# A scheduled attention and feed-forward kernel: a written order in place of a list scheduler, other places for the filler matmuls, and a last tile cut 384 and 128

## The chip, the core and the metric

The kernel runs on one core of a Trainium2 chip. The metric is the device time of one execution in microseconds (us); lower is better. Engines are named as the profile names them: PE is TensorE, PEld its weight loads, DVE is VectorE, ACT is ScalarE, POOL is GpSimd, SP is SyncE, which here only issues transfers.

## What is computed

Eight batches of eight heads, 576 tokens of 64 numbers each, go through two attentions and a feed-forward layer. First the 32 learned queries `p` attend to `k` and `v`; then `q` attends to the 32 results. The heads are laid side by side to a matrix of 4608 tokens by 512, which goes through `w_in` (512 by 2048), an activation and `w_out` (2048 by 512).

```python
def sm_attn(qq, kk, vv):
    s = scale * np.matmul(qq, kk.transpose(0, 1, 3, 2))
    a = np.exp(s - np.max(s, axis=-1, keepdims=True))
    a = a / (np.sum(a, axis=-1, keepdims=True) + 1e-09)
    return np.matmul(a, vv)
p_packed = sm_attn(p, k, v)
x = heads_side_by_side(sm_attn(q, p_packed, p_packed))
h = x @ w_in
g = np.where(h >= 1, h, np.where(h <= -1, 0.0, (h + 1) ** 2 / 4))
out = g @ w_out
```
(`heads_side_by_side` stands for a transpose and a reshape.)

## The kernel before

**The stages.** Each batch goes through the same steps, in tiles whose names are those of the profile. `tp` transposes `k` and `q` on PE for batches 0 and 1; later batches use DMA transposes that SP issues (`kT`, `qT`, L626). `sp` are the scores of `p`, `ex` their exponentials (ACT), `pk` the packed values and their sums, `rs` a reciprocal (DVE), `ppT` the packed values as bf16. `s` are the scores of `q`, `eT` their exponentials (ACT), `sm` their sums, `ln` and `rc` the reciprocal by logarithm and exponential (ACT), `A` the normalized weights (DVE). `mp` is the packed values times `w_in`, and `M` its bf16 copy (ACT or DVE, L333), so that the feed-forward layer's first product is `h = A·M` (L939). Each batch has 16 blocks of 128 columns of `d_ff`, numbered `fi`, and each block makes `h`, then `x` (ACT, L945), `t` (DVE L953 or ACT L955) and `hT` (DVE, L960). The output `o` (L1030) adds up 16 matmuls, one for each `fi`, into a tile of 128 tokens by 512; `ob` is its copy (L333, ACT or DVE) and L1058 stores it, in two pieces, since a tile's tokens lie in two places of the output. Two batches share nine output tiles, so tile `o1.3` is tile 3 of the second pair. The very last tile, `o3.8`, is computed and stored as two halves of 256 columns.

**What sets the order.** Every step is a task of class `Plan` with the engines that could run it, a duration on each, the tasks that it depends on and the buffers that it takes. `run` is a list scheduler: at each turn it takes, over all engines, a ready task that can start first, among those within 0.05 us by the lowest rank, and a free choice of engine falls to whichever is free. Ranks are due times in table `RANKS`. The result is sorted by planned start, and the code of all tasks is issued in that order; each engine then runs its own instructions in that order, and waits where data or a buffer is not there yet. PSUM slots for `h`, `mp`, `s`, `sm`, `tp` and `sp` come from a pool of three (`w`), those of `o` from a pool of two, and `ob` has four buffers.

**The filler matmuls.** Before the first `o`, PE is given matmuls on a tile of zeros (`o<-zeros`, L1108, 512 or 256 columns) in the planned gaps between its tasks. A list `fill` holds for each planned gap the planned time at which it begins and the number of matmuls, and the loop that issues the code puts them ahead of the first task, of any engine, that is planned to start later than that:

```python
    for t in order:
        while fill and t.start > fill[0][0] and t is not consts:
            warm(fill.pop(0)[1])
        t.ways[t.engine][2](t.engine)
```

Of the kernel before, what the change touches and what calls it, by code (L numbers as in the profile page):

```python
# [24 lines left out]
class Plan:  # L25
# [5 lines left out]
    CLAIM = 0.3  # L31
# [8 lines left out]
    def add(self, rank, ways, deps=(), takes=(), mode=None, behind=(), name=None, late=0.0):  # L40
        n = self.count[name]
        self.count[name] += 1
        if name in self.ranks:
            rank = float(self.ranks[name][min(n, len(self.ranks[name]) - 1)])
        t = Task(rank, ways, deps, takes, mode, behind, name, late)
        self.tasks.append(t)
        return t
# [7 lines left out]
    def run(self, slack):  # L55
        waiting = {id(t): len(t.deps) + len(t.behind) for t in self.tasks}
        for t in self.tasks:
            for d in t.deps + t.behind:
                d.users.append(t)
        ready = [t for t in self.tasks if not waiting[id(t)]]  # L60
        done = []
        while ready:
            best = None
            for claims in (True, False):
                found = defaultdict(list)
                left = {b: sorted(v) for b, v in self.slots.items()}
                for t in sorted(ready, key=lambda t: t.rank):
                    at = max((d.end + self.LATENCY for d in t.deps), default=0.0) + t.late
                    at = max([at] + [d.start + 0.001 for d in t.behind])
                    need = defaultdict(int)  # L70
                    for b in t.takes:
                        need[b] += 1
                    short = any(len(left[b]) < n for b, n in need.items())
                    wants = claims and at < self.free["PE"] + self.CLAIM
                    for b, n in need.items():
                        if not short:
                            at = max(at, left[b][n - 1] + self.LATENCY)
                        if wants:
                            del left[b][:n]
                    if short:  # L80
                        continue
                    for e in t.ways:
                        found[e].append((max(self.free[e], at), t))
                for e, some in found.items():
                    first = min(x[0] for x in some)
                    at, t = min((x for x in some if x[0] <= first + slack.get(e, 0.0)), key=lambda x: (x[1].rank, x[0]))
                    if best is None or at < best[0]:
                        best = at, t, e
                if best is not None:
                    break  # L90
            assert best is not None, "no step can take its buffers"
            at, t, e = best
            if e == "PE" and t.mode != self.mode:
                at = max(at, self.free[e] + self.SWITCH)
            ready.remove(t)
            keep, lasts = t.ways[e][:2]
            t.start, t.engine = at, e
            if e == "DMA":
                begin = max(self.pipe, at + lasts)
                self.pipe = begin + t.ways[e][3]  # L100
# [11 lines left out]
            if e == "PE":  # L112
                self.mode = t.mode
            for b in t.takes:
                self.slots[b].remove(min(self.slots[b]))
# [15 lines left out]
def kernel(  # L131
# [10 lines left out]
    nc = tc.nc  # L142
# [1001 lines left out]
```

## Time and profile before

| what | value |
|---|---|
| median of 3 runs | 241.63 us (241.58 to 241.64) |
| profiled execution, first to last instruction (span) | 240.4 us |
| median less span | 1.2 us |
| mean granted TensorE clock | 0.998 |
| PE busy | 233.2 us (97%) |
| ACT busy | 190.0 us (79%) |
| DVE busy | 179.4 us (75%) |
| POOL busy | 37.7 us (16%) |
| zero matmuls | 42, of them 36 of 512 columns and 6 of 256 |

The profiled execution shows its span alone; the time of a run holds 1.2 us more than that span, before the first instruction and behind the last. A share of busy time is an average over the whole span. The first 22 us are a start-up, in which loads land and the first batch goes through a chain of short steps; the rest is a steady stage in which PE alternates between `h` and `o`; the last microseconds are a copy and a store.

### The profile page before, as it was taken

The numbers are of one execution on the slowest core, as the hardware profiler recorded it, in microseconds if no ns is written. First come the engines' busy times: TensorE is split into PE (matmuls) and PEld (weight loads), VectorE is DVE, ScalarE is ACT, GpSimd is POOL, SyncE is SP. The second block draws the span as 40 slices with busy tenths as digits, with TensorE's granted clock in tenths as the row PEclk, the third lists the DMA queues.
The fourth block names the chain that finished last, engine by engine and source line by source line (L and its number), as shares of the span: only waits on it lengthen the run. The fifth ranks groups of instructions, "written<-read, shape, count | busy, mean of one in ns | idle before, by whom it ended". The sixth has DMA issues, their size and how long they took to land.

```text
span 240.4 us, 5315 instructions
## 1 busy us (share of the span) xinstructions
PE 233.2 (97%) x2096; PEld 133.9 (56%) x2096; DVE 179.4 (75%) x320; ACT 190.0 (79%) x324; POOL 37.7 (16%) x57
## 2 busy tenths in 40 slices
PE   7799999999999999999999999999999999999993
PEld 3555565565555655466546655656456554654452
DVE  4549997499977996699868989999469967995000
ACT  3578898799989986899889898998789886984211
POOL 8552306000510040070005000300000000000000
PEclk9999999999999999999999999999999999999999
DMA  7999999999999999999999997989301210111315
GB/s 155 201 206 207 203 202 206 199 257 171 148 188 248 186 171 204 187 174 213 204 183 197 218 213 117 138 189 203 97 2 48 74 33 27 44 40 52 98 45 119
DMA packets 65353, 36.42 MB, mean 152 GB/s; under 512 B 34480, under 2 KB 60848, under 8 KB 65328
## 3 DMA queue, kind: packets, MB, share of 16 engines
q0 software_dynamic: 28080, 18.26, 53.5%
q1 hardware_dynamic: 36544, 17.28, 33.4%
q10 hardware_dynamic: 704, 0.56, 0.8%
q8 instruction: 16, 0.26, 0.4%
q14 instruction: 9, 0.07, 0.1%
HBM read 37.22 MB, written 9.44 MB: 194 GB/s over the span
## 4 chain that ended last, share of the span: by engine, by line
PE 92%; ACT 3%; DMA 2%; DVE 1%; issue 0%
PE o L1030 51%; PE h L939 26%; PE mp L792 3%; DMA k_raw<-in_k_dram 2%; PE o L1108 2%; PE pk L730 2%; PE sm L835 2%; PE sp L652 2%; PE s L770 1%; PE tp L564 1%; ACT M L333 1%; PE pk L740 1%; DVE M L333 0%; ACT rc L846 0%; PE tp L601 0%; PE sp L667 0%
## 5 line engine op out<-in xcount | busy, mean ns | idle before, releaser
L1030 PE MATMUL o<-w_out_sb,hT 128*128 128x512 bf16 (+1 forms) x592 | 146.3, 374 | 0.0
L960 DVE SCALAR_TENSOR_TENSOR hT<-t 128x576 bf16<-128x576 f32 (+1 forms) x130 | 91.9, 742 | 3.7 <-ACT t L955 2.1
L945 ACT ACTIVATE x<-h 128x576 f32<-128x576 f32 (+1 forms) x130 | 79.2, 646 | 11.6 <-PE h L939 10.7
L1030 PEld LDWEIGHTS <-hT 128*128 128x128 bf16 x592 | 55.3, 98 | 49.3 <-issue 5.6
L939 PE MATMUL h<-A,M 128*128 128x288 bf16 x512 | 78.1, 286 | 0.6 <-ACT M L333 0.4
L939 PEld LDWEIGHTS <-M 128*128 128x128 bf16 x512 | 49.6, 98 | 27.7 <-issue 1.5
L953 DVE TENSOR_SCALAR t<-x 128x576 f32<-128x576 f32 (+1 forms) x75 | 33.6, 463 | 10.6 <-ACT x L945 10.2
L955 ACT ACTIVATE t<-x 128x576 f32<-128x576 f32 (+1 forms) x55 | 37.0, 684 | 0.9
L333 ACT COPY ob<-o 128x512 f32<-128x512 f32 (+1 forms) x21 | 11.9, 567 | 16.5 <-PE o L1030 16.3
L851 DVE SCALAR_TENSOR_TENSOR A<-eT,rs,rc 128x576 bf16<-128x576 bf16 (+1 forms) x18 | 12.9, 747 | 10.7 <-ACT rc L846 10.7
L333 ACT CAST M<-mp 128x1024 bf16<-128x1024 f32 (+1 forms) x19 | 17.7, 969 | 2.5 <-PE mp L792 2.4
L430 POOL DMA_DIRECT2D v<-in_v_dram x14 | 10.2, 731 | 52.2 <-DVE vz L708 48.9
L430 POOL DMA_DIRECT2D kz<-in_k_dram x14 | 9.7, 701 | 50.9 <-DMA kT<-kz 50.2
L333 DVE CAST M<-mp 128x1024 bf16<-128x1024 f32 (+1 forms) x15 | 17.2, 1147 | 0.4 <-PE mp L792 0.4
L333 DVE COPY ob<-o 128x512 f32<-128x512 f32 x16 | 10.9, 685 | 2.7 <-PE o L1030 2.6
L1108 PE MATMUL o<-zeros 128*128 128x512 bf16 (+1 forms) x42 | 11.4, 405 | 1.2 <-DVE zeros L367 1.2
L828 ACT ACTIVATE eT<-s,rs 128x576 bf16<-128x576 f32 x16 | 11.1, 736 | 1.8 <-PE s L770 1.2
L841 ACT ACTIVATE ln<-sm 128x576 f32<-128x576 f32 x16 | 10.1, 651 | 1.9 <-PE sm L835 1.7
L846 ACT ACTIVATE rc<-ln 128x576 f32<-128x576 f32 (+1 forms) x18 | 10.6, 634 | 0.0
L792 PE MATMUL mp<-w_in_sb,ppT 64*32 64x512 bf16 x256 | 10.3, 380 | 0.0
L674 ACT ACTIVATE ex<-sp 128x640 bf16<-128x640 f32 x14 | 9.5, 702 | 0.3 <-PE sp L652 0.2
L444 POOL DMA_DIRECT2D q<-in_q_dram x11 | 8.4, 762 | 5.1 <-ACT x L945 2.1
(62 smaller groups left out, 110.7 us busy)
## 6 DMA issues: line engine op xcount, KB each, us to landing
out_dram<-ob SPq DMA_DIRECT2D x23, 192.0 KB, 2.7
q<-in_q_dram POOLq DMA_DIRECT2D x7, 576.0 KB, 16.1
out_dram<-ob SPq DMA_DIRECT2D x24, 128.0 KB, 3.9
kz<-in_k_dram POOLq DMA_DIRECT2D x7, 320.0 KB, 6.4
v<-in_v_dram POOLq DMA_DIRECT2D x7, 320.0 KB, 8.6
w_out_sb<-in_moe_w_out_dram POOLq DMA_DIRECT2D x4, 512.0 KB, 15.3
kz<-in_k_dram POOLq DMA_DIRECT2D x7, 256.0 KB, 7.3
v<-in_v_dram POOLq DMA_DIRECT2D x7, 256.0 KB, 9.6
```

Source lines behind the costliest of these rows:

```text
L333: i = (nc.vector.tensor_copy if e == "DVE" else nc.scalar.copy)(to, of)
L430: return G_.dma_start(tokens(nm, b)[p0:p0 + R5, :, :c * D], of)
L792: i = nc.tensor.matmul(have["mp", b, f][a * NP:(a + 1) * NP, g], have["ppT", b][r, g, a], w_in_sb[r, a, f * FW:(f + 1) * FW], start=True, ...
L828: nc.scalar.activation(have["eT", b, g][:, part], have["s2", b, g][:, part, :HALF], AF.Exp, scale=rs_of[b][:, g, 1:])
L851: V.scalar_tensor_tensor(have["A", b][:, g, part], have["eT", b, g][:, part], rs_of[b][:, g, :1], have["rc", b, g][:, part], ALU.mult, ALU ...
L939: nc.tensor.matmul(have["h", b, fi][:, hf, :HALF], have["M", b][:, g, fi * P:(fi + 1) * P], have["A", b][:, g, hf], start=(g == 0), stop=( ...
L945: nc.scalar.activation(have["x", b, fi][:, hs[0]:hs[-1] + 1], have["h", b, fi][:, hs[0]:hs[-1] + 1, :HALF], AF.Prelu, bias=-1.0, alpha=0.5)
L953: V.tensor_scalar(t, x, 1.0, 0.0, ALU.add, ALU.max)
L955: nc.scalar.activation(t, x, AF.Relu, bias=1.0)
L960: V.scalar_tensor_tensor(dst, t, 1.0, t, ALU.min, ALU.mult)
L1030: m = nc.tensor.matmul(have["o", key][:, :w], hT[:, fi, i * P:(i + 1) * P], w_out_sb[:, fi, cols], start=(fi == 0), stop=(fi == KF - 1))
L1108: nc.tensor.matmul(o[:, :w], zeros[:, :P], zeros[:, :w], start=True, stop=True)
```

## The change

**The order.** `RANKS` now holds for every task a whole number, its place in the order, and for `x`/`t`/`hT` blocks, casts and copies a letter, `a` for ACT and `v` for DVE. `run` sorts the tasks by that number and takes the engine of the letter. It still walks through the tasks to give each a planned start, but that is used only to size and place the zero matmuls. A task's planned start no longer rises along the order, while the loop that places the zero matmuls (L1063 to L1066) is the same.

**The table's times.** Some durations and megabytes that the plan counts with are changed (`MB0`, `MB1`, loads, constants, casts).

**The last tile** has columns 384 and 128 in place of 256 and 256, and five early stores (`HALVED`) are issued as two of 256 columns each.

In the changed kernel line numbers are 50 or 51 lower from the copy helper on (L333 is now L282, `A` L851 is L801, `h` L939 is L889, `x` L945 is L895, `t` L953 and L955 are L903 and L905, `o` L1030 is L980); the store L1058 is L1010, and the zero matmuls L1108 are L1061.

```diff
-    def run(self, slack):
...
-                for e, some in found.items():
-                    first = min(x[0] for x in some)
-                    at, t = min((x for x in some if x[0] <= first + slack.get(e, 0.0)), key=lambda x: (x[1].rank, x[0]))
...
-        return sorted(done, key=lambda t: t.start)
+    def run(self):
+        order = sorted(self.tasks, key=lambda t: t.rank)
+        for t in order:
+            e = t.engine = t.engine or next(iter(t.ways))
+            at = max((d.end + self.LATENCY for d in t.deps), default=0.0) + t.late
+            at = max([at, self.free[e]] + [d.start + 0.001 for d in t.behind])
...
+        return order
...
-    MB0 = {("k", 0, 4): 1.17, ("v", 0, 0): 1.35, ("q", 0, 0): 0.3, ("q", 0, 4): 0.27, ("q", 0, 1): 0.27, ("q", 0, 5): 0.27}
-    MB1 = {("w_in", 0, 0): 0.52, ("w_in", 0, 1): 0.76}
+    LASTW, HALVED = (384, 128), {(1, 1, 0), (1, 1, 1), (1, 3, 0), (1, 3, 1), (1, 5, 0)}
+    MB0 = {("k", 0, 4): 1.42, ("v", 0, 0): 1.01, ("q", 0, 0): 0.28, ("q", 0, 4): 0.308, ("q", 0, 1): 0.3, ("q", 0, 5): 0.344}
+    MB1 = {("w_in", 0, 0): 0.466, ("w_in", 0, 1): 0.956, ("w_in", 1, 0): 0.94}
...
+        "M0.0.0": "65", "Mc0.0.0": "66v", "M0.0.1": "67", "Mc0.0.1": "68", "M0.1.0": "86", "Mc0.1.0": "87v", "Mc0.1.1": "88a", "M0.2.0": "121",
...
             def store(e, key=key, c0=c0, w=w):
                 for n_, (a, n, dst) in enumerate(rows):
-                    (nc.scalar if parts > 1 and n_ % 2 else nc.sync).dma_start(dst[:, cols], have["ob", key][a:a + n, :w])
...
+                    step = w // 2 if (pr, i, n_) in HALVED else w
+                    for x in range(0, w, step):
+                        (nc.scalar if parts > 1 and n_ % 2 else nc.sync).dma_start(dst[:, c0 + x:c0 + x + step],
+                                                                                  have["ob", key][a:a + n, x:x + step])
...
-            parts = 2 if (b, first + j) == (B - 1, 8) else 1
-            output(b // 2, first + j, start, span / KF / parts, parts)
+            widths = LASTW if (b, first + j) == (B - 1, 8) else (d_model,)
+            output(b // 2, first + j, start, span / KF / len(widths), widths)
...
-    order = plan.run({"PE": 0.05, "ACT": 0.05, "DVE": 0.05, "SP": 0.0, "DMA": 0.0})
+    order = plan.run()
```

**How rows move: PE at batch 0.** In the kernel before, PE goes from the second pair of `sm` matmuls straight to the eight `mp` (first rows of each shown), and zero matmuls follow behind them.

```order
L835 LDWEIGHTS onesblk
L835 MATMUL sm<-eT,onesblk 128x288
L792 LDWEIGHTS ppT
L792 MATMUL mp<-w_in_sb,ppT 32x512
...
L1108 LDWEIGHTS zeros
L1108 MATMUL o<-zeros 128x512
```

In the changed kernel, between the same `sm` and `mp` on PE, zero matmuls stand ahead of `mp`; the pair of rows on zeros is there eight times.

```order
L785 LDWEIGHTS onesblk
L785 MATMUL sm<-eT,onesblk 128x288
L1061 LDWEIGHTS zeros
L1061 MATMUL o<-zeros 128x512
...
L742 LDWEIGHTS ppT
L742 MATMUL mp<-w_in_sb,ppT 32x512
```

So the zero matmuls have moved from behind `mp`, where there were nine, to a place ahead of it. Behind `mp` PE now has two `h`, one and a half zero matmuls and six more `h`.

Shortly before, in the changed kernel, PE has zero matmuls also between the last transposes of `q` and the first scores `s` (`s_328` is the scores' tile of the first half of batch 0).

```order
L514 LDWEIGHTS q
L514 MATMUL tp<-ident,q 128x96
L1061 LDWEIGHTS zeros
L1061 MATMUL o<-zeros 128x512
L1061 LDWEIGHTS zeros
L1061 MATMUL o<-zeros 128x512
L1061 LDWEIGHTS zeros
L1061 MATMUL o<-zeros 128x256
L720 LDWEIGHTS ppT
L720 MATMUL s_328<-qT,ppT 32x288
```

In the kernel before, the first `s` stood between the third and the fourth group of transposes, with no zero matmul ahead of it; now both scores stand behind all transposes and 2.5 zero matmuls.

**DVE at batch 0.** The kernel before has on DVE, from the packed values to the first blocks of `h`:

```order
L333 CAST ppT<-pk 64x128 x2
L760 RECIPROCAL rs<-pk 128x4
L333 COPY qT<-tp 128x288 x5
L851 SCALAR_TENSOR_TENSOR A<-eT,rs,rc 128x288
L333 CAST M<-mp 128x512
L851 SCALAR_TENSOR_TENSOR A<-eT,rs,rc 128x288 x3
L953 TENSOR_SCALAR t<-x 128x288
```

The changed kernel has at that place on DVE:

```order
L710 RECIPROCAL rs<-pk 128x4
L282 CAST ppT<-pk 64x128 x2
L282 COPY qT<-tp 128x288 x6
L282 CAST M<-mp 128x512
L801 SCALAR_TENSOR_TENSOR A<-eT,rs,rc 128x288 x4
L903 TENSOR_SCALAR t<-x 128x288 x2
```

The reciprocal has moved ahead of the two casts, and the cast of `M` ahead of all four `A`.

**ACT at batch 1.** Before the first `h` of batch 1, ACT has in the kernel before two casts of `M` in a row:

```order
L841 ACTIVATE ln<-sm 128x576 x2
L846 ACTIVATE rc<-ln 128x576 x2
L333 CAST M<-mp 128x2x512 x2
L945 ACTIVATE x<-h 128x576 x7
L955 ACTIVATE t<-x 128x576 x2
```

In the changed kernel ACT has there:

```order
L791 ACTIVATE ln<-sm 128x576 x2
L796 ACTIVATE rc<-ln 128x576 x2
L282 COPY ob<-o 128x512
L282 CAST M<-mp 128x2x512
L282 COPY ob<-o 128x512
L895 ACTIVATE x<-h 128x576 x8
```

One cast of `M` stays on ACT, between two copies of `o`; the other is on DVE, and PE has ten `o` matmuls between `mp` and the first `h`. At batch 7 the order gives three of four casts of `M` to ACT, with ten `o` matmuls ahead of the first `h`. In all, eight `t` move from ACT to DVE, three casts of `M` go from DVE to ACT, and three copies of `o` go from ACT to DVE.

**SP around the transposes of batch 4.** With numbered tiles, SP has before:

```order
L1058 DMA out_0_dram<-ob_1603 96x512
L1058 DMA out_0_dram<-ob_1603 32x512
L626 DMA_TRANSPOSE kT_1645<-kz_78 128x20x128
L626 DMA_TRANSPOSE qT_1723<-q_1154 128x24x96
L1058 DMA out_0_dram<-ob_1634 96x512
L1058 DMA out_0_dram<-ob_1634 32x512
L1058 DMA out_0_dram<-ob_1817 64x512 x2
```

And in the changed kernel at that place on SP:

```order
L576 DMA_TRANSPOSE kT_1717<-kz_78 128x20x128
L576 DMA_TRANSPOSE qT_1719<-q_1240 128x24x96
L1010 DMA out_0_dram<-ob_1430 64x512 x2
L1010 DMA out_0_dram<-ob_1593 96x512
L1010 DMA out_0_dram<-ob_1593 32x512
L1010 DMA out_0_dram<-ob_1631 96x256 x2
L1010 DMA out_0_dram<-ob_1631 32x256 x2
L1010 DMA out_0_dram<-ob_1313 96x512
L1010 DMA out_0_dram<-ob_1313 32x512
L1010 DMA out_0_dram<-ob_1821 32x512
```

Behind the two transposes stand now the stores of four `ob` tiles (of them one in halves) ahead of that of a fifth, where there were the stores of two tiles.

## Rows read from the trace of the kernel before

**Rows 1.** Page, part 1: busy time, share of the span, number of instructions.

```profile
PE 233.2 (97%) x2096; PEld 133.9 (56%) x2096; DVE 179.4 (75%) x320; ACT 190.0 (79%) x324; POOL 37.7 (16%) x57
```

**Rows 2.** Timeline, PE, 46 to 52: start, length, instructions, [idle before <-releaser].

```profile
48.40 0.82 PE L1030 MATMUL o<-w_out_sb,hT 128*128 128x512 bf16 x3
49.40 0.65 PE L939 MATMUL h<-A,M 128*128 128x288 bf16 x4 [0.18 <-ACT M L333]
50.31 1.88 PE L939 MATMUL h<-A,M 128*128 128x288 bf16 x14 [0.26 <-ACT M L333]
```

**Rows 3.** Timeline, ACT, 46 to 52.

```profile
48.35 1.91 ACT L333 CAST M<-mp 128x1024 bf16<-128x1024 f32 x2
```

**Rows 4.** Timeline, all engines, 199 to 204.5.

```profile
201.83 1.47 PE L1030 MATMUL o<-w_out_sb,hT 128*128 128x512 bf16 x6
202.15 1.22 DVE L333 CAST M<-mp 128x1024 bf16<-128x1024 f32 x1
...
203.42 0.65 PE L939 MATMUL h<-A,M 128*128 128x288 bf16 x4
```

**Rows 5.** Timeline, PE, 11 to 23.

```profile
11.40 0.94 PE L735 MATMUL pk<-ex,v 96*64 96x32 bf16 x48
...
13.69 0.41 PE L564 MATMUL tp<-ident,q 96*128 96x96 bf16 x6 [0.23 <-DVE rs L760]
14.06 0.32 PE L770 MATMUL s<-qT,ppT 64*32 64x288 bf16 x8
...
17.36 0.41 PE L792 MATMUL mp<-w_in_sb,ppT 64*32 64x512 bf16 x8
17.70 2.01 PE L1108 MATMUL o<-zeros 128*128 128x512 bf16 x9
19.55 0.65 PE L939 MATMUL h<-A,M 128*128 128x288 bf16 x4
20.13 0.41 PE L792 MATMUL mp<-w_in_sb,ppT 64*32 64x512 bf16 x8
...
21.41 1.64 PE L939 MATMUL h<-A,M 128*128 128x288 bf16 x12
```

**Rows 6.** Timeline, ACT, 8 to 23.

```profile
9.48 1.50 ACT L676 ACTIVATE ex<-sp 96x768 bf16<-96x768 f32 x2 [0.20 <-PE sp L667]
...
14.45 0.74 ACT L828 ACTIVATE eT<-s,rs 128x576 bf16<-128x576 f32 x1
```

**Rows 7.** Timeline, DVE, 11 to 23.

```profile
17.84 0.69 DVE L333 CAST M<-mp 128x512 bf16<-128x512 f32 x1
18.45 1.51 DVE L851 SCALAR_TENSOR_TENSOR A<-eT,rs,rc 128x288 bf16<-128x288 bf16 x3
```

**Rows 8.** Timeline, ACT, 235 to 241: the last copy.

```profile
236.69 0.37 ACT L333 COPY ob<-o 128x256 f32<-128x256 f32 x1 [1.33 <-PE o L1030]
```

**Rows 9.** Tile `ob`, 236 to 241: the last stores.

```profile
DMA to landing us min/median/max: 1.8/1.9/2.0
```

**Rows 10.** Tile `ob`, 200 to 241: copies on DVE.

```profile
L333 DVE COPY ob<-o x2: 681/682/683, 213.4 to 215.1; 128x512 f32<-128x512 f32 x2
```

**Rows 11.** Timeline, SP, 94 to 110.

```profile
99.48 2.97 SPq L626 DMA_TRANSPOSE qT<-q  x1
102.54 7.67 SPq L1058 DMA_DIRECT2D out_dram<-ob  x5
```

**Rows 12.** Tile `ob`, 100 to 110: its stores.

```profile
DMA to landing us min/median/max: 4.8/5.9/6.3
```

**Rows 13.** Timeline, ACT, 106 to 110: the copies of `o`.

```profile
107.81 0.59 ACT L333 COPY ob<-o 128x512 f32<-128x512 f32 x1
```

**Rows 14.** Windows: busy time of PE, PEld, DVE, ACT, POOL; granted clock, DMA share, GB/s.

```profile
6.00:7.00 1.00, 0.00 (x0) 0.00 (x0) 0.51 (x1) 0.23 (x1) 1.00 (x3) 1.00 1.31 200
7.00:8.00 1.00, 0.60 (x10) 0.46 (x11) 0.10 (x1) 0.60 (x1) 0.33 (x1) 1.00 1.31 202
```

**Rows 15.** Timeline, PE, 0 to 10: the first zero matmuls.

```profile
1.19 3.22 PE L1108 MATMUL o<-zeros 128*128 128x512 bf16 x8 [1.19 <-DVE zeros L367]
```

More of the change, by code (lines that the diff above doesn't have):

```diff
@@ L30 @@
     SWITCH = 0.095
-    CLAIM = 0.3
+    LETTER = {"a": "ACT", "v": "DVE"}
     def __init__(self, buffers, ranks):
@@ L42, in add @@
         self.count[name] += 1
+        t = Task(rank, ways, deps, takes, mode, behind, name, late)
         if name in self.ranks:
-            rank = float(self.ranks[name][min(n, len(self.ranks[name]) - 1)])
-        t = Task(rank, ways, deps, takes, mode, behind, name, late)
+            r = self.ranks[name][n]
+            t.engine = self.LETTER.get(r[-1])
+            t.rank = int(r.rstrip("av"))
         self.tasks.append(t)
@@ L53, in release @@
             u.frees.append(box)
-    def run(self, slack):
[L56 to L83, printed above, removed]
-                for e, some in found.items():
-                    first = min(x[0] for x in some)
-                    at, t = min((x for x in some if x[0] <= first + slack.get(e, 0.0)), key=lambda x: (x[1].rank, x[0]))
[L87 to L92, printed above, removed]
@@ L96, in run @@
             keep, lasts = t.ways[e][:2]
-            t.start, t.engine = at, e
+            t.start = at
             if e == "DMA":
-                begin = max(self.pipe, at + lasts)
-                self.pipe = begin + t.ways[e][3]
+                self.pipe = max(self.pipe, at + lasts) + t.ways[e][3]
                 t.end = self.pipe + t.ways[e][4]
@@ L397, in held @@
                     mybir.DependencyClass.Sync, mybir.DependencyReason.DATA), reason="a load begun behind another has landed")
-        t = plan.add(rank, {"DMA": (0.78, 2.1, held, mb / 0.405, settle)}, hold, takes=list(takes) + ["dma"])
+        t = plan.add(rank, {"DMA": (0.78, 2.1, held, mb / 0.405, settle)}, hold, takes=list(takes) + ["dma"], name="load")
         plan.release("dma", [t])
@@ L1033, in mm @@
                         apart(m, both, i, "mm")
-                t = plan.add(rank + pitch * (fi + KF * part), {"PE": (0.2158 / parts, 0.165 + 0.215 / parts, mm)},
+                t = plan.add(rank + pitch * (fi + KF * part), {"PE": (0.2158 * w / FW, 0.165 + 0.215 * w / FW, mm)},
                              [t for b in bs for t in g_of[b, fi]] + [landed["w_out", fi // Q]],
@@ L1047, in output @@
             last = rank + pitch * KF * (part + 1)
-            c = plan.add(last, {"ACT": (0.52, 0.585, out_copy), "DVE": (0.65, 0.68, out_copy)}, [t], ["ob"], name=f"o{pr}.{i}")
+            c = plan.add(last, {"ACT": (0.1 + 0.42 * w / FW, 0.165 + 0.42 * w / FW, out_copy), "DVE": (0.13 + 0.52 * w / FW, 0.16 + 0.52 * w / FW, out_copy)}, [t], ["ob"], name=f"o{pr}.{i}")
             if both:
@@ L1054, in output, with store @@
                 plan.release("w" if lent else "o", [c])
[L1056 removed]
+            def store(e, key=key, c0=c0, w=w):
                 for n_, (a, n, dst) in enumerate(rows):
[L1058 to L1060 removed]
+                    step = w // 2 if (pr, i, n_) in HALVED else w
+                    for x in range(0, w, step):
+                        (nc.scalar if parts > 1 and n_ % 2 else nc.sync).dma_start(dst[:, c0 + x:c0 + x + step],
+                                                                                  have["ob", key][a:a + n, x:x + step])
+            st = plan.add(last + 0.01, {"SP": (0.4 * (len(rows) + sum((pr, i, n_) in HALVED for n_ in range(2))), 3.0, store, 0.85 * w / FW, 0.0)}, [c], name=f"o{pr}.{i}")
             plan.release("ob", [st])
```

46 lines of the change are left out of this document (19 added, 27 removed), and 214 rows, old and new, of the table RANKS.

## The prediction

> **What bounds the kernel now.** I read the busy times first: PE has 233.2 of 240.4 us, ACT and DVE far less [rows 1]. A kernel whose PE is busy for 97% can gain only where PE waits, where it runs matmuls that compute nothing, and behind its last matmul. So the timeline of PE is next, read for places where a row starts later than the one before it lets go. The pitch of `o` is (1.47 − 0.82)/3 = 0.217 us, from a row of six and one of three [rows 2, 4]; that of `h` is (1.88 − 0.65)/10 = 0.123 [rows 2]. Once `o` has begun PE is late at three places:
>
> - batch 1: three `o` from 48.40 let go at 49.05 and `h` starts at 49.40, 0.35 late; four `h` let go at 49.89 and the next start at 50.31, 0.42 late [rows 2]. Both wait for the two casts of `M` that stand in a row on ACT, 1.91 us [rows 3];
> - batch 7: six `o` from 201.83 let go at 203.13, `h` starts at 203.42, 0.29 late, behind a cast of `M` on DVE that ends at 203.37 [rows 4].
>
> That is 1.06 us in all. The rest of the steady stage is PE work that both kernels have alike. What is left is the start-up to the twelve `h` at 21.41 [rows 5], from which PE runs without a break, and the tail: a copy from 236.69 for 0.37 [rows 8], an issue, and a landing after 1.9 [rows 9].
>
> The sum is made against the span of 240.4; the 1.2 us between it and the median of 241.63 are taken as unchanged.
>
> **The start-up, step by step.** Here the order changes most, so I walk through it with the old durations in the new order.
>
> *To the scores.* `pk` starts at 11.40, after seven zero matmuls, though `ex` ended at 9.48 + 1.50 = 10.98 [rows 5, 6]. The changed order has four zero matmuls there, so `pk` can start at about 11.0: −0.4. The third group of `q` transposes stands 2.29 behind `pk` [rows 5]; that carries it to 13.29, the fourth group 0.37 later (the step from 13.69 to 14.06), its end to 14.03. Then come 2.5 zero matmuls that weren't there, 2.5 × 0.217 = 0.54, and only then `s`: about 14.5 against 14.06, +0.45 in spite of the early `pk`. That the reciprocal goes ahead of the casts of `ppT` on DVE costs its own length, under 0.2, and is covered by those transposes and zeros.
>
> *To `mp`.* `eT` follows `s` by 0.39 and lasts 0.74 [rows 5, 6]. Both `s` now stand together, so the second `eT` follows the first at once: 14.9 to 15.65 and to 16.3; the second `sm` runs to about 16.65. Before, `mp` came right behind that `sm`, at 17.36, and nine zeros behind it [rows 5]. Now eight zeros, 8 × 0.217 = 1.74, stand ahead of it: `mp` at about 18.45, +1.1.
>
> *To `h`.* The cast of `M` follows `mp` by 0.48 (17.36 to 17.84) and lasts 0.69 [rows 5, 7]: on DVE 18.93 to 19.6. Before, one `A` went ahead of it and three behind, in 1.51 with a wait for `rc` among them [rows 7]; I take 0.45 each. Now all four stand behind the cast, and end at about 21.35. Before, `h` was held by the nine zeros alone (17.70 + 9 × 0.206 = 19.55, where it starts) [rows 5], well covered; that cover is gone, since the zeros have been spent ahead of `mp`. The first blocks of `h` then need each `A` as it comes, the next `mp` starts at 21.85, and the `h` that stood at 21.41 [rows 5] come 0.34 later, at 22.2. **Head: +0.8.** Four zero matmuls fewer of 512 columns (33 and 4 of 256, for 36 and 6, is four columns' worth of 512) would be −0.87 if they were what binds; they aren't, since they only shorten a stretch that now ends on `A`.
>
> **The steady stage.** At batch 1 one of the two casts is on DVE and ten `o` (2.17 us) stand ahead of `h`; a cast begun 0.48 behind `mp` and behind a copy of 0.59 [rows 13], with 0.96 of its own (half of 1.91 [rows 3]), is done after 2.03, so nothing is late. At batch 7 three casts on ACT are 2.9 us, but the first `h` needs one of them, behind ten `o`. So both waits go: −1.06. An order written from a plan's times has waits of its own where a duration is a tenth off, and with eight `t` more on DVE, DVE is closer to the path. The three waits in the old order are 0.29 to 0.42 each; one such, **+0.35**, is what I put in, with 0 and 1.06 as its ends.
>
> The five stores in halves cost SP one more issue each, off the path unless SP is late (a rival below).
>
> **The tail.** The PE work of the last tile is the same, 512 columns 16 times. The last copy is of 128 columns on DVE; no row has that. Its upper bound is ACT's 0.37 for 256 columns [rows 8]; DVE takes 0.68 for 512 [rows 10], a quarter of which, 0.17, is the lower bound. I take 0.28, nearer the middle, since part of such a copy doesn't shrink: −0.09. The last store has a quarter of a tile, where it had half: between no gain and 0.3 of 1.9 [rows 9]; I take −0.1, for most of a landing doesn't depend on size. The store of the 384 columns is issued some 0.9 us (16 × 0.054) ahead of that copy, and its landing could now be the later one; this is why I don't take more. **Tail: −0.19.**
>
> **Sum.** +0.8 − 1.06 + 0.35 − 0.19 = −0.1: span 240.3, time **241.5**. A difference of under 0.2% (0.48 us) is about what a measurement of this kernel can't tell from no change, so this counts as the same.
>
> **Rivals.**
>
> *The head gains instead (faster).* The step that carries my loss is that zeros ahead of `mp` delay everything behind. If PE got past them sooner than I think, or `h` were bound by `eT`, `ln` and `rc` on ACT rather than by `mp`, `mp` could come at 16.9, 1.55 sooner, and the `h` of 21.41 at 20.65: head −0.76. For it: `A` in the old order waits for `rc`, not for `M`. Against: PE runs its rows in order, and the zeros are in its row. −0.76 − 1.06 + 0.35 − 0.19 = −1.66: about 240.0.
>
> *The written order is cleaner than I assume.* No new wait, and the tail's gains at their bounds (−0.2 and −0.3): +0.8 − 1.06 − 0.5 = −0.76: about 240.9.
>
> *Stores hold `ob` (slower).* One mechanism at one place: around the transposes of batch 4, stores of four `ob` tiles queue on SP behind the transposes, and there are four `ob` buffers, so a fifth copy waits for the first landing. In the old trace the last transpose is issued at 99.48 for 2.97, the stores follow at 102.54 [rows 11] and land 4.8 to 6.3 later [rows 12]: 107.3 to 108.8. Copies of `o` start at 107.81 [rows 13], so the margin is from +0.5 to −1.0. If the fifth copy is due by 107.8 and the landing comes at 108.8, PE's next `o` has no PSUM slot for 1 us: +1.0, about 242.5. It decides once landing is later than the copy plus what the second `o` slot covers. For it: landings are far longer there than at the end (5.9 to 1.9 [rows 9, 12]). Against: the old order had stores at this place too without holding any copy.
>
> *The waits stay.* If the casts at batch 1 are late anyhow (the copy ahead on ACT and `A` ahead on DVE push them by 0.8), the old 0.77 there comes back: −0.1 + 0.7 = +0.6, about 242.2.
>
> *The clock.* PE now has pauses of some 0.7 us (before the second half's `sm`) and 1.2 us (between `mp` and `h`) at which no zero matmul stands. In the old trace PE does nothing from 6 to 7, and the granted clock is 1.00 in that window and in the next [rows 14]: the full level, 2.4 GHz, and no fall. Were it to fall to the 1.2 GHz level, the first zeros show the price: eight in 3.22 [rows 15], 0.40 each where 0.217 is the pitch, so about 1.5 us: 243.0. The Trainium skill says on page "TensorE: Matmul & The Clock Gate", section "HAM oscillation — how this bites in real kernels", that idle gaps of the matmul engine let its clock gate fall back to half, which is what zero matmuls are there to prevent; by that rule alone the change, which spends them at the wrong place, would pay the 243.0. The trace agrees with the rule only for the start of the kernel (slow zeros after an idle 1.19 us before the first) and speaks against it for the pause from 6 to 7.
>
> **Chances.** My forecast 0.52, own range 241.1 to 241.9 (no new wait, or 0.7 of them); cleaner 0.14; head gains 0.10; `ob` held 0.13; waits stay 0.07; clock 0.04. Faster than 241.15: 0.14 + 0.10 and a small part of the forecast's own (0.04): 0.28. Slower than 242.11: 0.13 + 0.04 and half of the waits' 0.07, rounded to 0.20. Same: 0.52. The range leaves out the head's gain (0.10) and, above, the clock with half of the stores' case (0.10): 240.6 to 242.4.
>
> **What would show it.** In the changed kernel's trace: `pk` at about 11.0; `s` at about 14.5, with 2.5 zeros ahead; `mp` at 18.4, behind eight zeros; the first `A` behind the cast of `M`, and the `h` ahead of the second `mp` with waits for DVE; a break-free PE from 22.2. If `mp` comes at 17.5 or sooner, or `h` runs on from 20.7, the head is wrong. At batch 1 and 7 `h` should follow the last `o` by no more than a pitch. A wait of a copy for a DMA near 107 to 109 would be the stores' rival, a granted clock below 1.00 at 15 to 22 the clock's. The last copy should take about 0.28, and the last landing under 1.9. A wait of PE over 0.3 anywhere between 23 and 236 that isn't at the places named makes my steady stage wrong.

## The result and the profile after

The changed kernel takes 242.84 us (median of 7 runs, 242.27 to 243.58), the old one 241.58 (7 runs, 241.26 to 241.96): ratio 1.0048, 95% interval 1.0038 to 1.0058. It is slower by 0.5%. I had forecast 241.5, and 242.84 lies above my range. The profiled execution of the changed kernel took 242.84 us with a span of 241.1.

The part of the page on busy time has to be read with care here:

```profile
PE 230.6 (96%) x2057; PEld 133.0 (55%) x2091; DVE 181.1 (75%) x328; ACT 187.7 (78%) x316; POOL 38.2 (16%) x57
```

There are 2091 weight loads and 2057 matmuls: 34 records of matmuls are missing, so that PE's 230.6 us is no gain over [rows 1], and a count of matmuls in a row below can be one short of the order's.

The start-up comes first. PE, timeline from 11 to 24:

```profile
11.18 0.94 PE L685 MATMUL pk<-ex,v 96*64 96x32 bf16 x48
...
14.73 0.44 PE L720 MATMUL s<-qT,ppT 64*32 64x288 bf16 x16
...
16.83 1.89 PE L1061 MATMUL o<-zeros 128*128 128x512 bf16 x8
18.65 0.41 PE L742 MATMUL mp<-w_in_sb,ppT 64*32 64x512 bf16 x8
20.27 0.71 PE L889 MATMUL h<-A,M 128*128 128x288 bf16 x2 [1.21 <-DVE A L801]
...
22.05 0.65 PE L889 MATMUL h<-A,M 128*128 128x288 bf16 x4 [0.50 <-ACT x L895]
22.63 0.41 PE L742 MATMUL mp<-w_in_sb,ppT 64*32 64x512 bf16 x8
22.97 1.28 PE L889 MATMUL h<-A,M 128*128 128x288 bf16 x9
```

Eight zero matmuls hold PE for 1.8 us, with `mp` behind them; then `h` waits 1.21 us for `A`. The `h` that stood at 21.41 in [rows 5] starts at 22.97. The two waits between have their reason on DVE and ACT, timelines of the same stretch:

```profile
19.10 0.69 DVE L282 CAST M<-mp 128x512 bf16<-128x512 f32 x1 [4.28 <-PE mp L742]
19.71 1.79 DVE L801 SCALAR_TENSOR_TENSOR A<-eT,rs,rc 128x288 bf16<-128x288 bf16 x4
...
21.59 0.41 ACT L895 ACTIVATE x<-h 128x288 f32<-128x288 f32 x1 [0.16 <-PE h L889]
```

DVE stands idle for 4.28 us in front of the cast, with the four `A` behind it. The wait at 22.05 is for the `x` that ends at 22.00.

The two places at which the old kernel was late [rows 2, 4] are clean. PE from 48 to 53 and from 199 to 204.5:

```profile
49.69 1.03 PE L980 MATMUL o<-w_out_sb,hT 128*128 128x512 bf16 x4 [0.16 <-issue]
50.55 2.61 PE L889 MATMUL h<-A,M 128*128 128x288 bf16 x20
...
200.37 2.55 PE L980 MATMUL o<-w_out_sb,hT 128*128 128x512 bf16 x11
202.75 2.00 PE L889 MATMUL h<-A,M 128*128 128x288 bf16 x15
```

No `h` waits for a cast of `M`. (At the 0.16 a record is missing: five weight loads stand there for four matmuls.) The reason is another than the text of the change and the prediction have it: at batch 1 five `o` stand between `mp` and the first `h`, not ten, and at batch 7 eleven. PEld and ACT at batch 1:

```profile
49.46 0.76 PEld L980 LDWEIGHTS <-hT 128*128 128x128 bf16 x5 [0.42 <-issue]
49.66 1.02 ACT L282 CAST M<-mp 128x1024 bf16<-128x1024 f32 x1
```

The first `h` starts at 50.55, while ACT's cast still runs (to 50.68), so it does not wait for that cast at all.

But there is a new place, batch 5, at 137 to 142. On DVE, ACT and PE:

```profile
135.71 3.43 DVE L910 SCALAR_TENSOR_TENSOR hT<-t 128x576 bf16<-128x576 f32 x5
...
139.43 0.17 DVE L710 RECIPROCAL rs<-pk 128x4 f32<-128x4 f32 x1
139.52 0.56 DVE L282 CAST ppT<-pk 64x128 bf16<-64x128 f32 x2
...
139.63 0.53 ACT L282 CAST ppT<-pk 64x128 bf16<-64x128 f32 x2 [1.54 <-DVE rs L710]
...
140.50 0.71 PE L720 MATMUL s<-qT,ppT 64*32 64x288 bf16 x16
141.44 0.41 PE L742 MATMUL mp<-w_in_sb,ppT 64*32 64x512 bf16 x8 [0.23 <-ACT x L895]
```

`rs` now stands ahead of the casts of `ppT`, on DVE behind a row of `hT`. ACT waits 1.54 for it, the second half of `s` waits for ACT, and `mp` for the `x` that ACT is late with. The kernel before has the casts first, and its DVE is free there and waits for `pk`. DVE and PE of that kernel:

```profile
138.12 0.60 DVE L333 CAST ppT<-pk 64x128 bf16<-64x128 f32 x2 [0.34 <-PE pk L740]
138.75 0.18 DVE L760 RECIPROCAL rs<-pk 128x4 f32<-128x4 f32 x1
...
139.39 0.44 PE L770 MATMUL s<-qT,ppT 64*32 64x288 bf16 x16
139.65 0.40 PE L792 MATMUL mp<-w_in_sb,ppT 64*32 64x512 bf16 x8
```

From the first `s` to `mp` the changed kernel takes 0.94, the one before 0.26. The loss is 0.68.

The end, ACT and DVE from 233 on:

```profile
236.92 0.48 ACT L282 COPY ob<-o 128x384 f32<-128x384 f32 x1 [2.01 <-PE o L980]
...
237.81 0.29 DVE L282 COPY ob<-o 128x128 f32<-128x128 f32 x1 [9.71 <-PE o L980]
```

The last matmul starts at 237.55, the last store lands at 240.08, and the span ends at 241.07.

### The profile page after: what moved, and what is told of

The parts are those of the page before. It is cut to its first block, busy times and chain, and to the rows that moved or that the text cites. A ratio compares the mean times of both kernels' runs of the same rounds, so it can differ in the third digit from the quotient of the medians.

```text
span 241.1 us, 5273 instructions
## 1 busy us (share of the span) xinstructions
PE 230.6 (96%) x2057; PEld 133.0 (55%) x2091; DVE 181.1 (75%) x328; ACT 187.7 (78%) x316; POOL 38.2 (16%) x57
## 4 chain that ended last, share of the span: by engine, by line
PE 86%; DMA 3%; DVE 3%; issue 2%; ACT 2%; POOL 2%; ACTq 0%; POOLq 0%
PE o L980 50%; PE h L889 24%; PE mp L742 4%; DMA q<-in_q_dram 3%; PE sm L785 2%; DVE hT L910 2%; PE sp L602 2%; PE pk L680 1%; PE o L1061 1%; PE s L720 1%; ACT x L895 1%; DVE t L903 1%; POOL q L393 1%; PE tp L514 1%; PE pk L690 1%
## 5 line engine op out<-in xcount | busy, mean ns | idle before, releaser
L980 PE MATMUL o<-w_out_sb,hT 128*128 128x512 bf16 (+2 forms) x560 | 137.5, 373 | 2.1 <-issue 0.8
L895 ACT ACTIVATE x<-h 128x576 f32<-128x576 f32 (+1 forms) x130 | 78.1, 643 | 12.0 <-PE h L889 10.8
L980 PEld LDWEIGHTS <-hT 128*128 128x128 bf16 x592 | 54.9, 98 | 51.8 <-issue 5.7
L889 PE MATMUL h<-A,M 128*128 128x288 bf16 x512 | 75.9, 286 | 2.1 <-DVE A L801 1.2
L889 PEld LDWEIGHTS <-M 128*128 128x128 bf16 x512 | 49.4, 98 | 26.5 <-DVE M L282 1.1
L903 DVE TENSOR_SCALAR t<-x 128x576 f32<-128x576 f32 (+1 forms) x84 | 36.9, 454 | 12.3 <-ACT x L895 11.9
L905 ACT ACTIVATE t<-x 128x576 f32<-128x576 f32 x46 | 31.0, 683 | 0.7
L282 DVE COPY ob<-o 128x512 f32<-128x512 f32 (+1 forms) x20 | 13.4, 668 | 19.7 <-PE o L980 19.7
L282 ACT CAST M<-mp 128x1024 bf16<-128x1024 f32 (+1 forms) x22 | 20.7, 974 | 2.5 <-PE mp L742 2.4
L282 ACT COPY ob<-o 128x512 f32<-128x512 f32 (+1 forms) x17 | 9.8, 575 | 14.1 <-PE o L980 13.8
L282 DVE CAST M<-mp 128x1024 bf16<-128x1024 f32 (+1 forms) x12 | 13.6, 1130 | 5.9 <-PE mp L742 5.9
L801 DVE SCALAR_TENSOR_TENSOR A<-eT,rs,rc 128x576 bf16<-128x576 bf16 (+1 forms) x18 | 12.7, 745 | 2.7 <-ACT rc L796 2.7
L1061 PE MATMUL o<-zeros 128*128 128x512 bf16 (+1 forms) x35 | 11.2, 445 | 1.3 <-DVE zeros L316 1.2
```

The lines of the kernel that those rows point to most:

```text
L282: i = (nc.vector.tensor_copy if e == "DVE" else nc.scalar.copy)(to, of)
L801: V.scalar_tensor_tensor(have["A", b][:, g, part], have["eT", b, g][:, part], rs_of[b][:, g, :1], have["rc", b, g][:, part], ALU.mult, ALU ...
L889: nc.tensor.matmul(have["h", b, fi][:, hf, :HALF], have["M", b][:, g, fi * P:(fi + 1) * P], have["A", b][:, g, hf], start=(g == 0), stop=( ...
L895: nc.scalar.activation(have["x", b, fi][:, hs[0]:hs[-1] + 1], have["h", b, fi][:, hs[0]:hs[-1] + 1, :HALF], AF.Prelu, bias=-1.0, alpha=0.5)
L903: V.tensor_scalar(t, x, 1.0, 0.0, ALU.add, ALU.max)
L905: nc.scalar.activation(t, x, AF.Relu, bias=1.0)
```

## The experiments

All were compared with runs of the old kernel between theirs (median 241.55 to 241.67 in the four groups).

| kernel | median us (lowest to highest) | ratio to the old kernel, 95% |
|---|---|---|
| old, again | 241.55 (241.39 to 242.16) | 1.0003 (0.9994 to 1.0011) |
| changed, zeros at the gaps | 243.88 (242.23 to 245.62) | 1.0096 (1.0058 to 1.0134) |
| changed, `A` ahead of `M` | 242.54 (242.06 to 245.90) | 1.0033 (1.0020 to 1.0045) |
| changed, `rs` of batch 5 behind | 241.95 (241.63 to 243.03) | 1.0023 (1.0009 to 1.0036) |
| changed, three mended | 241.50 (240.31 to 242.46) | 0.9995 (0.9977 to 1.0012) |
| old, last tile alone | 241.62 (241.12 to 242.51) | 1.0006 (0.9994 to 1.0019) |
| old, zeros ahead of `mp` | 243.14 (242.91 to 243.48) | 1.0073 (1.0061 to 1.0085) |
| changed, no zeros behind `pk` | 243.44 (242.38 to 243.79) | 1.0075 (1.0057 to 1.0094) |
| changed, whole stores | 243.69 (242.88 to 244.51) | 1.0078 (1.0056 to 1.0100) |
| three mended, `v` of batch 4 later too | 240.70 (240.22 to 241.86) | 0.9958 (0.9942 to 0.9974) |
| the same, whole stores, `h` in other order | 241.66 (240.49 to 242.13) | 0.9991 (0.9977 to 1.0005) |
| changed, `h` in other order | 242.29 (241.89 to 242.94) | 1.0024 (1.0012 to 1.0035) |
| `v` later too, `h` in other order | 241.22 (240.05 to 242.79) | 0.9984 (0.9965 to 1.0004) |
| old, with the five halves | 241.52 (241.13 to 242.11) | 1.0000 (0.9991 to 1.0010) |

**The old kernel again.**

> The kernel before, unchanged, run again to have its span in several executions. In the changed kernel a run's time is 1.77 us more than its span in each of seven runs (242.84 and 241.1, 242.27 and 240.5). If that is so in the old kernel too, its usual span is about 239.8 (241.58 less 1.77), its profiled 240.4 was a long execution, and the change costs 1.26 within the span. If its spans are 240.4 here too, the old kernel has only 1.2 us outside the span, and half a microsecond of the loss is outside.

In eleven runs its time is 1.75 to 1.85 us more than its span (241.39 and 239.6, 242.16 and 240.4; spans stand on record to 0.1 us), as in the changed kernel. So its usual span is 239.8, and the 240.4 on whose rows I predicted was a long execution. Its `k_raw` landed at 6.74, and at 5.97 in this one. The twelve `h` of [rows 5], then at 21.41, start at 20.63 here:

```profile
18.77 0.65 PE L939 MATMUL h<-A,M 128*128 128x288 bf16 x4
19.36 0.41 PE L792 MATMUL mp<-w_in_sb,ppT 64*32 64x512 bf16 x8
...
20.63 1.65 PE L939 MATMUL h<-A,M 128*128 128x288 bf16 x12
```

**The place of the zero matmuls, from both sides.** In the changed kernel each gap's zeros are put directly ahead of the PE task that the gap precedes; in the old one the eight and a half behind the first `mp` are put ahead of it.

```diff
(changed kernel)
-        while fill and t.start > fill[0][0] and t is not consts:
-            warm(fill.pop(0)[1])
+        if id(t) in fill:
+            warm(fill[id(t)])
(old kernel)
+    early = max(fill, key=lambda x: x[1] * (x[0] > 12))
+    fill.remove(early)
+    ahead = next(t for t in order if t.name == "M0.0.0")
...
+        if t is ahead:
+            warm(early[1])
```

> The changed kernel with the same zero matmuls, each directly ahead of the PE task before which the plan has the gap (eight of them behind the first or last mp instead of ahead, 2.5 behind the first s instead of ahead). Theory Z, the place of the zeros carries the loss of the start-up: the first s at 14.3 (14.73), the first mp at about 16.5 (18.65), the twelve h behind the second mp at about 21.0 (22.97), time 241.3 (1.2 to 2.0 less than 242.84). Rival D, the cast of M ahead of all A on DVE carries it: mp comes early but A and h stay where they are within 0.4, time 242.4 or more.

> The old kernel with the eight and a half zero matmuls of the gap behind the first mp moved ahead of it; nothing else. Theory Z: mp 1.85 later (18.4 for 16.6), of which 0.9 was covered by the zeros that h waited for, so the twelve h start about 1.0 later (21.6 for 20.63) and the time is 0.7 to 1.2 more: 242.5. Rival: zeros that stand there cost nothing, since h waits for A and not for M: within 0.2 of 241.55.

With the zeros at the gaps, `mp` starts at 15.99 and the `h` of 22.97 at 20.62. Counted from `pk`, that is 10.03 us (10.59 to 20.62), as in the old kernel (10.01, from 10.62 to 20.63), where the changed one has 11.79: the start-up's loss is gone. The time did not fall to the 241.3 expected; it rose to 243.88. Part of the reason stands below. In the old kernel the zeros alone cost 1.58 us (243.14 for 241.56), more than the 0.7 to 1.2 expected. PE there:

```profile
18.50 0.41 PE L792 MATMUL mp<-w_in_sb,ppT 64*32 64x512 bf16 x8
19.74 0.30 PE L939 MATMUL h<-A,M 128*128 128x288 bf16 x1 [0.82 <-DVE M L333]
20.59 0.53 PE L939 MATMUL h<-A,M 128*128 128x288 bf16 x3 [0.55 <-DVE A L851]
...
22.32 1.64 PE L939 MATMUL h<-A,M 128*128 128x288 bf16 x12
```

`mp` is 1.92 later than in the old kernel's own trace (16.58), `h` 1.69. Theory Z holds in both kernels, and its rival (zeros cost nothing there) falls.

What PE met 2 us earlier, in the changed kernel with zeros at the gaps, is batch 2. PE from 62 to 70 and SP and POOL from 55 on:

```profile
64.53 0.76 PE L602 MATMUL sp<-pT,kT 128*128 128x64 bf16 x20 [0.32 <-DMA kT<-kz]
...
69.48 0.44 PE L720 MATMUL s<-qT,ppT 64*32 64x288 bf16 x16 [0.76 <-DMA qT<-q]
```
```profile
55.58 3.00 SPq L576 DMA_TRANSPOSE kT<-kz  x1
58.69 6.76 SPq L576 DMA_TRANSPOSE qT<-q  x1
```
```profile
56.74 1.71 POOL L379 DMA_DIRECT2D v<-in_v_dram  x2 [16.46 <-DVE vz L658]
```

POOL begins to load `v` of batch 3 as soon as DVE has copied `v` of batch 2, right behind the issue of `kT`, which then takes 8.9 us to land (64.49). In the trace of the old kernel run again `v` is loaded from 61.90, and `kT`, issued at 56.50, lands after 5.1 (61.55). The two waits are 1.08 us, in the shortest of six runs (242.23); what the long ones lost, up to 245.62, is not shown.

**No zeros behind `pk`.**

```diff
-            warm(fill.pop(0)[1])
+            at, n = fill.pop(0)
+            if at < 11.5:
+                warm(n)
```

> The changed kernel without any zero matmul behind pk (17 of 512 and 3 of 256 columns fewer), which leaves PE pauses between s, sm, mp and h. Theory Z: the granted clock stays at 1.00 and the first h comes as soon as M and A allow, the twelve h at 20.6 or a little sooner, for 22.97 in the changed kernel; then the same scattered waits at batch 2 as with the zeros at the gaps, 242 to 244. Rival, the clock: with pauses of a microsecond the granted clock falls below 1.00 between 16 and 24 and h runs at more than 0.122 us each; the twelve h at 21 or later.

The rival is right here. Windows of that kernel (columns as in [rows 14]) and its PE:

```profile
14.00:15.00 1.00, 0.77 (x16) 0.28 (x4) 0.47 (x2) 0.77 (x2) 0.46 (x1) 1.00 1.28 218
15.00:16.00 1.00, 0.75 (x4) 0.30 (x3) 0.00 (x0) 1.00 (x2) 0.69 (x1) 0.74 1.20 197
16.00:17.00 1.00, 0.97 (x10) 0.22 (x8) 0.12 (x1) 0.81 (x3) 0.00 (x0) 0.50 1.23 204
```
```profile
21.51 4.02 PE L889 MATMUL h<-A,M 128*128 128x288 bf16 x16
```

After pauses of 0.31, 0.27 and 0.20 between the transposes, `s` and `sm` the clock falls to 0.50 (the 1.2 GHz level) and comes back only between 25 and 26. Sixteen `h` take 4.02 us, where the kernel with zeros at the gaps has 2.13. So in the trace the zeros hold the clock, and it is their place that costs. The time, 243.44 on four runs, can't be told from that with the zeros at the gaps (243.88). In the changed kernel as it is, the clock stays: 1.00 in these windows of its start-up, in which PE has its waits of 1.21 and 0.50:

```profile
18.00:20.00 2.00, 1.06 (x12) 0.31 (x11) 0.90 (x2) 1.52 (x5) 0.69 (x2) 1.00 1.24 206
20.00:22.00 2.00, 1.14 (x6) 0.58 (x6) 1.77 (x5) 0.91 (x3) 0.13 (x2) 1.00 1.24 206
```

**`A` ahead of `M`.**

```diff
-"A0.0.0": "71" ... "Mc0.0.0": "66v"
+"A0.0.0": "66" ... "Mc0.0.0": "71v"
```

> The changed kernel with the first A ahead of the cast of M on DVE, as in the old order (A, M, A x3); the zeros stay at their new places. Theory Z: the first A runs at 18.1 while DVE waited, the last one ends 0.45 sooner (21.0 for 21.5), so 0.3 to 0.5 less: 242.4. Rival D: it gives back most of the start-up's loss: 1.0 or more less, 241.8 or under.

The median is 0.30 less, as theory Z had it, but the two intervals overlap; what the run rules out is rival D's 1.0 or more. It isn't a clean test: the loop places zeros by planned starts, and with this order there are nine and a half zeros ahead of `mp`, not eight.

**The order of `h`.**

```diff
-"h0.0": "78 79 80v 81 82 83 89v 90", "h0.1": "75 76 77v 98 84 85 97v 100"
+"h0.0": "78 79 80v 81 84 85 89v 90", "h0.1": "75 76 77v 98 82 83 97v 100"
```

> The changed kernel with the second halves of the first two blocks of h in the other order (first block's second half last); nothing else. In the changed kernel h at 22.05 waits 0.50 for ACT's x of the first half of the same block, since both halves lie in one PSUM tile and the written order puts x between. Theory: that wait goes or shrinks to 0.1, the second mp comes at 22.2 for 22.63, 0.3 to 0.5 less: 242.4. Rival: h waits there for A (the last A ends at 21.5): 0.1 or less, 242.8.

The wait shrinks from 0.50 to 0.16, and the time by 0.55. The second `mp` comes 0.49 sooner (22.14 for 22.63), but the first one was already 0.25 sooner in that execution (18.40 for 18.65), so the order of `h` shows for 0.24 of it:

```profile
21.80 0.41 PE L889 MATMUL h<-A,M 128*128 128x288 bf16 x2 [0.16 <-ACT x L895]
22.14 0.41 PE L742 MATMUL mp<-w_in_sb,ppT 64*32 64x512 bf16 x8
```

**`rs` of batch 5.**

```diff
-"pp5.0": "867v", "pp5.1": "866a", "rs5": "865"
+"pp5.0": "865v", "pp5.1": "866a", "rs5": "867"
```

> The changed kernel with the reciprocal rs of batch 5 behind the casts of ppT, as in the old order, and not ahead of them. Theory R, at 139 to 141 s is late because ACT's cast of ppT waits for rs, which stands on DVE behind five hT: ACT casts at 138.2 instead of 139.63, s follows at about 140.0 instead of 140.50, and the 0.78 us that PE loses at 140.5 shrinks to 0.2 or 0.3; time 0.4 to 0.6 less, 242.3. Rival: s waits for DVE's own cast behind the hT, whatever stands in front of it: PE still loses 0.6 or more, time within 0.2 of 242.84.

The order on PE is the same, and 0.89 us are gone (241.95 for 242.84), more than the 0.4 to 0.6 expected. ACT and PE of that kernel:

```profile
138.03 0.53 ACT L282 CAST ppT<-pk 64x128 bf16<-64x128 f32 x2 [0.21 <-PE pk L690]
```
```profile
140.22 0.44 PE L720 MATMUL s<-qT,ppT 64*32 64x288 bf16 x16
140.48 0.40 PE L742 MATMUL mp<-w_in_sb,ppT 64*32 64x512 bf16 x8
```

ACT casts 1.60 earlier, and `mp` stands 0.26 behind `s`. DVE's own casts are at 139.15 and in time. The trace shows 0.68 of the 0.89, and 0.68 is more than half of the 1.26 that the change lost.

**Mending.** Zeros at the gaps and `rs` behind, with the copies of `v` of batch 2 later in the order; then those of batch 4 too; then the other order of `h`, once with whole stores.

```diff
-"vv2.0": "306", "vv2.1": "326"
+"vv2.0": "351", "vv2.1": "352"
(and in the next)
-"vv4.0": "614", "vv4.1": "615"
+"vv4.0": "645", "vv4.1": "646"
```

> The changed kernel with three things mended: the zero matmuls at the gaps, rs of batch 5 behind the casts of ppT, and the two copies of v of batch 2 (vz on DVE) 25 to 45 places later in the order. The zeros at the gaps alone brought the start-up back to the old kernel's (20.62) but left two waits of PE for transposes of batch 2 at 64 and 69, 0.3 and 0.8 us, with runs from 242.2 to 245.6. Theory L, that stage waits for transfers since PE comes 2 us sooner and v of batch 3 is loaded from 56.7 instead of 61.9, beside the transposes: with vz later kT lands within 6 us of its issue, no wait at 64, runs within 0.5 of each other, time about 240.3, faster than both kernels. Rival: transfers are late there whatever the copies of v do: the waits stay, time 241.5 to 243 and scattered.

> The kernel with three things mended (241.5, from 240.31 to 242.46) and the copies of v of batch 4 (vz) some 30 places later, so that v of batch 5 is loaded later than 101.3. There a copy of o at 108.7 waits for a store issued at 101.25 that lands at 108.65, 7.4 us later, beside those loads; PE loses about 0.5. Theory L: with the loads later the store lands in under 6.5 us, no wait of the copy, 0.4 to 0.6 less and less scatter: 241.0. Rival: the stores are late from their own number (ten issues in a row): landing and wait stay, within 0.2 of 241.5.

> The same, with whole stores in place of halves and with the second halves of the first two blocks of h in the other order, so that h does not wait for the x of its own first half. If stores are late from their number, three issues fewer bring the landing forward and the wait at 108.7 goes here and not in the kernel with v later alone. The other order of h gives 0.2 to 0.4 in the start-up. 240.6 to 240.9, faster than both kernels; if transfers rule the stage whatever is done, 241.2 or more.

> The kernel of 240.70 (zeros at the gaps, rs of batch 5 behind, copies of v of batches 2 and 4 later, halves kept) with the second halves of the first two blocks of h in the other order, which alone gave 0.55 in the changed kernel. If the wait for x is what it saved there, the start-up is 0.2 to 0.3 shorter here too, where the wait is 0.23: 240.4. If what it saved is given back at the stores of batch 4, since PE comes sooner: 240.7.

With `v` later `kT` lands 5.2 us after its issue and the waits at 64 and 69 are gone, as theory L has it, but the time was 241.5 and not 240.3, and scattered. The slower rival of my prediction stands at batch 4 now. PE with three mended, then with `v` of batch 4 later too:

```profile
108.52 0.59 PE L980 MATMUL o<-w_out_sb,hT 128*128 128x512 bf16 x2
109.39 0.81 PE L980 MATMUL o<-w_out_sb,hT 128*128 128x512 bf16 x3 [0.27 <-ACT ob L282]
```
```profile
108.54 1.31 PE L980 MATMUL o<-w_out_sb,hT 128*128 128x512 bf16 x5
```

In the first a copy waits for a store that was issued at 101.25 and landed at 108.65. In the second no `o` waits, and the kernel takes 240.70, faster than the old one by 0.42% (interval 0.26 to 0.58) and than the changed one by 2.1 us. But theory L did not come as it was written. The store landed after 7.15 us (7.40 before), not under 6.5, and the copy still waits for it, 0.85 us on ACT:

```profile
108.40 0.58 ACT L282 COPY ob<-o 128x512 f32<-128x512 f32 x1 [0.85 <-DMA out_dram<-ob]
```

It comes 0.35 sooner than with three mended, and that is enough for PE not to wait. Of the 0.80 by which the time fell, this place shows 0.37 (from that `o` to the next `sp` 1.51 and 1.14); the rest is not shown.

The two further kernels gave nothing more. With whole stores and the other order of `h` (241.66, where 240.6 to 240.9 was forecast) the same store lands after 7.43 us, and PE waits 0.30 for a copy at 108.73: fewer stores did not bring the landing forward. With halves and the other order of `h` (241.22, for 240.4 or 240.7) the start-up is 0.5 shorter (20.46 for 20.98), of which 0.28 was there at the first `mp` already, and the wait of `o` at 109 is back, 0.31 at 109.48.

**The end.**

> The old kernel with the last tile as 384 and 128 columns, nothing else. The changed kernel ends 3.5 us after the start of its last matmul, the old one 4.0. If the widths give that by themselves: 0.4 to 0.5 less, 241.1. By my prediction's size, 0.19 less: 241.35. If the end is set by something else, 241.55.

> The changed kernel with whole stores in place of the five in halves; nothing else. The prediction's slower rival, stores that hold ob: in the changed kernel's trace no copy of o waits for a landing, so halves cost nothing and give nothing there: within 0.2 of 242.84. If the extra issues on SP held copies anywhere on the path, it is 0.3 or more faster; if halves bring landings forward on which something waits, slower.

> The old kernel with the same five stores in halves; nothing else. Leaving the halves out of the changed kernel cost 0.33 between the last matmul and the end in its trace, of which 0.3 from the last landing to the end (1.28 for 0.98), though no copy waits for a store. Theory E: five transfers more move the last two stores from the third and fourth to the last two of the nine semaphores that SP waits for in turn at the end, so the end comes 0.98 behind the last landing here too: 0.3 less, 241.3. Rival: halves act through the stores of batch 4, which hold no copy in the old kernel: 1.28 behind the landing, 241.6.

The edits are the two column widths in the old kernel; `HALVED = set()` in the changed one; the five halved stores in the old one. The last tile by itself gives nothing that can be measured (241.62 for 241.56). Whole stores cost 0.85 in the changed kernel by the medians, against the expectation of nothing. What the traces have of it, in us (read from the instructions' records):

```
kernel                    last matmul starts   last landing   span ends   landing to end
old, again                      235.61            238.33        239.61         1.28
old, last tile alone            235.94            238.52        239.81         1.29
old, with five halves           236.10            238.82        239.80         0.98
changed                         237.55            240.08        241.07         0.99
changed, whole stores           237.35            240.11        241.39         1.28
```

At the end SP waits in turn for nine pairs of semaphores, 0.06 us each when they are set. The last two stores have the third and fourth of them in the kernels with 1.28, and the eighth and ninth in those with 0.98; five transfers more or fewer move them on. So theory E holds for 0.3 in the trace. In the old kernel's time it doesn't show (241.52 for 241.62, within its interval). Of the 0.85 that whole stores cost, 0.33 is there in the traced execution (243.17 for 242.84). That is the difference of the whole, not that behind the last matmul, as the expectation has it: there it is 0.52 (4.04 for 3.52), 0.29 of it behind the landing, while PE was 0.20 sooner. Three of the six runs are at 242.9 to 243.2 and three at 244.2 to 244.5, the median lies between them, and what the long ones lost stays open.

## Why the prediction was wrong

The sum was a span of 240.3 and a time of 241.5; measured were 241.07 and 242.84. The miss of 1.34 is made of four terms (the end of the last matmul is its start and its columns' share of the pitch, 0.06 us for 128 and 0.11 for 256):

| term | forecast | measured | off by |
|---|---|---|---|
| twelve `h` of the start-up begin | 22.2 | 22.97 | +0.77 |
| from there to the end of the last matmul | 214.37 | 214.64 | +0.27 |
| from there to the end of the span | 3.73 | 3.46 | −0.27 |
| time less span | 1.2 | 1.77 | +0.57 |

**"The 1.2 us between it and the median of 241.63 are taken as unchanged" was the first failing step.** Time less span is 1.77 in both kernels; the 1.2 was never either's. The profiled 240.4 was 0.6 above the usual 239.8, and one execution's span was set against the median of others.

**"Head: +0.8" was the second: right in its mechanism, mis-sized.** Against the rows it was +1.56 (22.97 for 21.41). The walk held to `mp`: `pk` at 11.18 (11.0 forecast), `s` at 14.73 (14.5), `mp` behind eight zeros at 18.65 (18.45), the first `A` behind the cast of `M`. So 0.2 was missing at `mp`. Then "the first blocks of `h` need each `A` as it comes" left out that `h` also waits for `x`. Two halves of a block share a PSUM tile, and the written order puts the `x` of the first half ahead of the second: a wait of 0.50, of which the other order of `h` took away 0.34.

Like has to be set against like here too. In the changed kernel's profile `k_raw` landed at 6.91, as late as in the rows (6.74). With early landings (5.97 in both) the twelve `h` start at 20.63 in the old kernel and at 22.68 in the changed one with only `rs` of batch 5 moved: +2.05. An early landing gave the old start-up 0.78 and the new one 0.29.

**The steady stage.** −1.06 was right as a sum: both places are clean. Its reason was partly luck. The ten `o` that were to cover the cast at batch 1 are five, 1.09 us for 2.17, and a cast done 2.03 behind `mp` would have been late by that working; it didn't matter, since the first `h` did not wait for that cast. "+0.35" for waits of the new order's own was mis-sized; it was one loss of 0.68 in the trace, at batch 5. The mechanism was in my text, at batch 0 only: "the reciprocal goes ahead of the casts of `ppT`", with the price of "its own length, under 0.2". At batch 0, where DVE is free, its casts start 0.10 behind `rs` (12.64 for 12.54) and ACT's 0.22. At batch 5 DVE has a row of `hT` ahead of it, and another engine waits for the row.

**The tail.** −0.19 was forecast, and −0.46 to −0.43 came (3.46 for 3.92 in the old profile and 3.89 in the old kernel run again). The copy was right (0.29 for 0.28). The rest, 0.3, is no copy and no landing but the order in which the end waits for semaphores, which no term had.

**The rivals.** "The head gains instead" fell: `mp` came at 18.65, behind the zeros. "The waits stay" fell at batch 1, and "cleaner" at batch 5. "Stores hold `ob`" isn't in the changed kernel, whose PE comes late, but is the next bound as soon as PE comes in time. "The clock" stayed at 1.00 over pauses of 0.74, 1.21 and 0.50 us in the changed kernel, so the 243.0 priced for a fall was not paid, and that 242.84 lies near it is chance.

**What the change's steps are worth then.** Waits removed −1.1, `rs` +0.7, tail −0.45. The start-up is +1.6 to +2.05, by the landing; for the 1.26 measured from the old kernel's usual 239.8 it has to be about +2.1. That the sum closes is therefore no test of the start-up's size. The test is the old kernel with its zeros moved, +1.58.

## What to carry to other kernels

Fillers belong to the instruction that they precede, not to a time: when a list is no longer sorted by that time, a rule like "ahead of the first task that starts later" silently moves them ahead of work that others wait for, and only the order on the engine shows it. When a small step moves ahead on a busy engine, price it by the row that it stands behind there and by who waits on another engine, not by its length. Take time less span from one and the same execution before one profile is set against a median, and look for a landing that makes that execution special.

## What was not expected of the hardware

In the kernel without zeros behind `pk` the granted clock fell to 0.50 after three pauses of PE of 0.20 to 0.31 us between 12 and 15, and it stayed there through full windows of PE work until between 25 and 26. In the changed kernel waits of 0.74, 1.21 and 0.50, with zeros between them, did not do it. The Trainium skill, on page "TensorE: Matmul & The Clock Gate", section "HAM oscillation — how this bites in real kernels", has idle gaps as what makes the clock fall. This trace agrees in so far as taking the zeros out brought the fall; its pauses are far shorter than the waits for transfers in that section's example, and whether the pauses did it or the small matmuls between them is not shown.

The transpose of `k` for batch 2 landed after 5.1 to 5.4 us where two loads of `v` started behind its issue by 4.6 us or more, and after 8.9 where they started 1.2 behind it (55.58 and 56.74). Which semaphore the last stores fall on moved the end of the span by 0.3 us in the traces.
